# Other due times and ranks for the first five blocks of a fused retention and feed-forward kernel

## The chip, the cores and the metric

The kernel runs on one core of one Trainium2 chip. The metric is the device time of one execution in microseconds (us), the median over several runs. The profile shows one execution; in it PE is the matrix engine, DVE the vector engine, ACT the scalar engine, POOL the general engine, SP the engine that only issues DMAs, and a q behind an engine's name marks its instruction sequencer.

## The reference

```python
scores = scale * np.matmul(q, k.transpose(0, 1, 3, 2))        # 8 batches, 8 heads, 576 tokens, 64 wide
gamma = 1.0 - 2.0 ** (-5.0 - np.arange(H, dtype=np.float32))
rel = pos[:, None] - pos[None, :]
Dmat = np.where(rel >= 0, gamma[:, None, None] ** rel[None, :, :], 0.0)
attn = np.matmul(scores * Dmat[None], v)
x = attn.transpose(0, 2, 1, 3).reshape(4608, 512)
h = x @ w_in                                                  # 512 x 2048
g = np.where(h > 0.0, h, np.exp(np.minimum(h, 0.0)) - 1.0)
out = g @ w_out                                               # 2048 x 512
```

Inputs and output are float32; the kernel multiplies in bfloat16.

## The kernel before

**The work.** Retention runs in chunks of 64 tokens with a running state per head. The 4608 tokens are cut into items of 256 tokens. The four items of the first two batches are cut once more, into two halves by heads; these eight pieces are the units 0 to 7. Each unit has three loads, q, k and v (256 KB each): `ldq4`, `ldk4` and `ldv4` are those of unit 4. From them come scaled and cast copies (`cq` q times its decay, `kk` k cast, `vs` v times its decay), transposed operands, scores with a mask (`mask`), a state (`us`, `ub`) and the transposed input `xt` of the feed-forward part (`xc`). Units 0 to 4 are transposed by PE (`T4_0`, `T4_1`) and copied out of PSUM (`cp`); units 5 to 7 by a DMA transpose on SP's queue (`tr5`, `tr6`, `tr7`; line 594). `A4` to `A7` are the joined PE steps of units 4 to 7: scores and state of this unit, values of the one before.

**The feed-forward part** runs in blocks of 256 tokens. `F1_b_p` is eight matmuls of block b against `w_in`; ACT takes the exponential (`ex`), ACT or DVE the rectified half (`md`), DVE joins them (`g`); `F2_b_t_f` is four matmuls against `w_out`. Blocks 0 and 1 need units 0 to 3, block 2 units 4 and 5, block 3 units 6 and 7.

**The weights.** `w_in` comes in five DMAs (`wi0` to `wi4`, line 486) and `w_out` in four (`wo0` to `wo3`, 512 KB each in bfloat16, line 497), all issued by POOL, with a cast on the way. All other loads are issued by SP in one fixed order (line 392; one early load by ACT). Two loads are held until a quarter of `w_out` is there: POOL copies one element of that quarter into the load's target (line 403), and SP's load waits for this copy. As SP works in order, all loads behind `ldq4` wait with it.

```python
HOLD = {"ldq4": "wo0", "ldq6": "wo1"}
```

**The order.** A list of operations is laid out by a planner inside the kernel while it is built: each operation has a cost on each engine that can do it, a rank, and optionally a due time (`AT`, in us) before which the planner doesn't place it. The planner picks engine and order; the chip then runs each engine's instructions strictly in this order, held only by semaphores. Due times themselves don't exist on the chip. Where the planner sees a gap on PE in the first 50 us, it puts in dummy matmuls on zeros (`zero`, lines 280 and 1273) as filling.

Of the kernel before, what the change touches and what calls it, by code (L numbers as in the profile page):

```python
# [227 lines left out]
UAPART = (5, 7)  # L228
HOLD = {"ldq4": "wo0", "ldq6": "wo1"}
VLATE = (0, 1)  # L230
AT = {"wi0": 7.1, "wi1": 8.0, "wi2": 8.5, "wi3": 11.0, "wi4": 15.0, "wo0": 16.4, "wo1": 16.1, "wo2": 19.3, "wo3": 31.3, "so_0_1_0_0": 74, "so_1_0_0_0": 74, "so_1_1_0_0": 74, "so_2_0_0_0": 76, "so_2_1_0_0": 81.47, "F2_3_1_0_0": 78.57, "g_2_6": 63.17, "md_3_3": 66.87, "md_1_7": 35.82, "us5_0": 44.11, "ex_2_4": 55.85, "ex_2_2": 53.77, "xc1_u4": 43.93, "xc0_4": 82.16, "g_1_3": 27.7, "xc1_u3": 22.43, "F2_3_0_8_0": 78.02, "md_0_7": 36.11, "F1_6_6": 119.86, "tr0_5": 66.58, "md_2_2": 56.94, "ex_6_5": 119.61, "md_0_1": 21.97, "mask1_7": 117.16, "md_0_5": 25.96, "F2_4_0_8_0": 93.26, "cv7": 47.1, "F1_0_5": 22.04, "cq11": 5.73, "ub5_1": 47.68, "F1_0_3": 19.14, "g_1_7": 36.97, "vs1_7": 47.23, "cq00": 4.92, "cq16": 39.58, "ex_0_3": 22.04, "kk1_4": 33.96, "tr6": 42.78, "md_1_0": 25.42}
RANKS = {"us1_0": -2, "F1_0_1": 4, "mask0_7": 2, "g_2_1": -2, "md_3_3": 8, "A7": -4, "cv1_5": -4, "cv1_6": 4, "mask1_u6": 8, "so_5_0_0_0": -8, "md_0_2": -8, "ex_2_7": 2, "xc0_u7": -8, "F1_2_6": -8, "A4": 2, "F2_3_0_4_0": -8, "ub0_0": -4, "kk1_2": 4, "g_0_5": 4, "F2_1_1_0_0": 8}
FREE = ("f", "e", "em", "g", "ot")
SURE = 3
ATT = ((0, 0), (0, 1), (1, 0), (1, 1), (2, 0), (2, 1), (3, 0), (3, 1), (4, 0), (4, 1), "X",
# [12 lines left out]
def kernel(  # L248
# [997 lines left out]
    for op, name in holds:  # L1246
        op.deps.append(named[name])
    for name, t in AT.items():
        if name in named:
            named[name].early = t  # L1250
    for name, shift in RANKS.items():
        if name in named:
# [59 lines left out]
```

## Time and profile before

| what | us |
|---|---|
| median of 3 runs | 298.61 (298.08 to 298.75) |
| the profiled execution | 298.65 |
| its span, first to last instruction | 296.9 |
| PE busy in the span | 289.6 (98%) |
| DVE, ACT, POOL busy | 200.7, 160.1, 119.8 |

The profiled execution's own time is 1.75 us above its span; that part lies outside the instructions. A row of the timeline reads: start, duration, engine, line, operation, tiles, shapes, count, and in brackets the idle time before it with what ended it. A row of the windows gives for each stretch the busy time of each engine, then the clock granted to PE (1.00 is full), the mean busy share of the 16 DMA engines (it passes 1 where packets of several queues overlap) and GB/s. A row of the chain of waits gives start, duration and what the end of the program waited for then.

### The profile page before, as it was taken

How to read it: one execution, taken by the hardware profiler on the slowest of the kernel's cores; microseconds unless marked ns; L12 is line 12 of the kernel's file. 1: busy time of each engine (PE TensorE's matmuls, PEld its weight loads, DVE VectorE, ACT ScalarE, POOL GpSimd, SP SyncE). 2: the span in 40 equal slices, each digit the busy share in tenths (PEclk: the TensorE clock that was granted, in tenths of full speed). 3: DMA queues.
4: the chain of work that ended last, by engine and by line, in shares of the span. 5: the costliest groups of instructions: out<-in, count | busy, mean ns of one | idle time of the engine just before them, and what ended most of it. 6: DMA issues, size and time to landing. Idle time of an engine off the chain costs nothing.

```text
span 296.9 us, 9161 instructions
## 1 busy us (share of the span) xinstructions
PE 289.6 (98%) x3825; PEld 186.8 (63%) x3825; DVE 200.7 (68%) x374; ACT 160.1 (54%) x299; POOL 119.8 (40%) x193
## 2 busy tenths in 40 slices
PE   7999998999999999999999999999999999999995
PEld 4778644776585866776666677767666444444444
DVE  3878831987775878787786867767876567766500
ACT  5568615774283745656565466454565548544311
POOL 5932675763836544565456347370720000000000
PEclk9999999999999999999999999999999999999999
DMA  7999989999999985799999699976461100011221
GB/s 227 283 207 208 285 230 221 263 243 197 291 241 216 270 191 119 187 233 229 239 202 245 127 230 235 244 131 178 112 109 38 38 35 35 0 38 38 50 91 72
DMA packets 128618, 50.67 MB, mean 171 GB/s; under 512 B 92608, under 2 KB 124096, under 8 KB 128576
## 3 DMA queue, kind: packets, MB, share of 16 engines
q1 hardware_dynamic: 123296, 45.63, 67.4%
q0 software_dynamic: 4752, 4.19, 8.8%
q8 instruction: 30, 0.49, 0.7%
q10 hardware_dynamic: 528, 0.26, 0.3%
q14 instruction: 12, 0.10, 0.1%
HBM read 36.70 MB, written 9.44 MB: 155 GB/s over the span
## 4 chain that ended last, share of the span: by engine, by line
PE 82%; DMA 12%; POOL 3%; SPq 1%; issue 1%; ACT 0%; POOLq 0%; ACTq 0%
PE f L280 82%; DMA r<-in_q_dram 4%; DMA w_out_sb<-in_moe_w_out_dram 4%; DMA r<-in_v_dram 2%; DMA T<-st 2%; POOL w_in_sb L486 1%; POOL vn L582 1%; SPq L392 1%; POOL st L559 1%; SPq L594 0%; ACT ot L1179 0%; POOL r L403 0%; POOLq L559 0%; POOL pos_i L515 0%; ACTq L1179 0%
## 5 line engine op out<-in xcount | busy, mean ns | idle before, releaser
L280 PE MATMUL f<-xt,w_in_sb 128*128 128x256 bf16 (+1 forms) x1024 | 140.1, 286 | 0.3 <-DMA w_in_sb<-in_moe_w_in_dram 0.3
L280 PE MATMUL f<-w_out_sb,g 128*128 128x512 bf16 (+1 forms) x592 | 140.2, 373 | 0.0
L1118 ACT ACTIVATE e<-f 128x512 f32<-128x512 f32 x144 | 85.3, 598 | 76.1 <-PE f L280 74.7
L280 PEld LDWEIGHTS <-w_in_sb 128*128 128x128 bf16 x1024 | 99.4, 98 | 37.6 <-DMA w_in_sb<-in_moe_w_in_dram 0.6
L280 PEld LDWEIGHTS <-g 128*128 128x128 bf16 x592 | 56.7, 98 | 51.4
L1132 DVE TENSOR_SCALAR em<-e 128x512 bf16<-128x512 f32 x84 | 45.0, 538 | 39.5 <-ACT e L1118 39.5
L1142 DVE SCALAR_TENSOR_TENSOR g<-f,em 128x512 bf16<-128x512 f32 x84 | 57.4, 688 | 5.5
L1140 DVE SCALAR_TENSOR_TENSOR g<-e,f 128x512 bf16<-128x512 f32 x60 | 40.3, 681 | 10.0 <-ACT f L1128 9.0
L630 POOL CAST kv<-r 128x512 bf16<-128x512 f32 x28 | 17.0, 629 | 48.7 <-issue 26.5
L1179 ACT COPY ot<-f 128x512 f32<-128x512 f32 (+1 forms) x37 | 21.3, 576 | 26.5 <-PE f L280 26.2
L650 POOL TENSOR_TENSOR kv<-r,gq 128x512 bf16<-128x512 f32 x28 | 29.3, 1067 | 12.7 <-DMA r<-in_q_dram 12.7
L650 POOL TENSOR_TENSOR kv<-r,gk 128x512 bf16<-128x512 f32 x28 | 29.5, 1063 | 8.5 <-DMA r<-in_k_dram 8.5
L1128 ACT ACTIVATE f<-f 128x512 f32<-128x512 f32 x54 | 32.2, 598 | 0.0
L1001 ACT CAST xt<-f 128x512 bf16<-128x512 f32 (+1 forms) x36 | 20.7, 624 | 19.5 <-PE f L280 19.4
L969 DVE TENSOR_TENSOR pt<-f,mask 128x512 bf16<-128x512 f32 x28 | 18.0, 679 | 3.0 <-PE f L280 3.0
L954 POOL CAST bd<-S 128x256 bf16<-128x256 f32 x41 | 16.0, 405 | 9.8 <-ACT S L940 5.1
L942 DVE TENSOR_TENSOR S<-f,S 128x256 f32<-128x256 f32 x36 | 15.1, 419 | 3.2 <-PE f L280 1.2
L965 DVE TENSOR_TENSOR pt<-f,mask_u 128x512 bf16<-128x512 f32 x16 | 10.3, 682 | 8.5 <-PE f L280 8.5
L280 PEld LDWEIGHTS <-kv 64*64 64x64 bf16 x832 | 10.8, 104 | 0.1
L280 PE MATMUL f<-T 64*64 64x64 bf16 (+1 forms) x576 | 9.6, 199 | 1.2 <-DMA T<-st 1.2
L559 POOL TENSOR_TENSOR st<-r,gq 128x256 bf16<-128x256 f32 x14 | 8.8, 645 | 4.0 <-DMA r<-in_q_dram 3.9
L280 PEld LDWEIGHTS <-T 64*64 64x64 bf16 x576 | 7.3, 108 | 2.3 <-DMA T<-st 1.4
(67 smaller groups left out, 123.5 us busy)
## 6 DMA issues: line engine op xcount, KB each, us to landing
r<-in_v_dram SPq DMA_DIRECT2D x32, 256.0 KB, 4.5
r<-in_k_dram SPq DMA_DIRECT2D x31, 256.0 KB, 4.3
out_dram<-ot SPq DMA_DIRECT2D x31, 256.0 KB, 2.9
r<-in_q_dram SPq DMA_DIRECT2D x12, 512.0 KB, 4.6
r<-in_q_dram SPq DMA_DIRECT2D x8, 256.0 KB, 4.3
w_out_sb<-in_moe_w_out_dram POOLq DMA_DIRECT2D x4, 512.0 KB, 11.5
w_in_sb<-in_moe_w_in_dram POOLq DMA_DIRECT2D x3, 512.0 KB, 9.1
out_dram<-ot SPq DMA_DIRECT2D x10, 128.0 KB, 2.2
```

Of the source, the lines that this page charges most:

```text
L280: return pin(nc.tensor.matmul(*a, **kw))
L630: pin(copy[op.eng](heads(tiles[nkey][:, VS[s]]), tiles["rv", n][:, s * H : (s + 1) * H]))
L650: pin(alu[op.eng].tensor_tensor(tiles[nkey][:, 2 * i + j].rearrange("p (y x d) -> p x y d", y=2, x=HP), raw.rearrange("p (x y) d -> p x y ...
L954: pin(copy[op.eng](tiles[bkey], tiles[skey]))
L969: pin(nc.vector.tensor_tensor(pt.rearrange("p h s n -> p (h s) n"), src.rearrange("p (h n) -> p h n", n=C), mask.rearrange("p e r -> p (e ...
L1001: pin(copy[op.eng](dst, src))
L1118: pin(nc.scalar.activation(tiles[ekey], tiles[hkey], AF.Exp))
L1128: pin(nc.scalar.activation(ph, ph, AF.Relu))
L1132: pin(alu[op.eng].tensor_scalar_add(em, e, -1.0))
L1140: pin(nc.vector.scalar_tensor_tensor(g, e, -1.0, ph, ALU.add, ALU.min))
L1142: pin(nc.vector.scalar_tensor_tensor(g, ph, 0.0, tiles[mkey], ALU.max, ALU.min))
L1179: pin(copy[op.eng](tiles[okey][:, :width], tiles[pkey][:, :width]))
```

## The change

Only the two tables of due times and ranks differ, and of them only entries of the first five blocks and units 0 to 7. `HOLD` is as it was.

```diff
-AT: "wi2": 8.5, "wo0": 16.4, "wo1": 16.1, "wo2": 19.3, "wo3": 31.3, "F1_0_3": 19.14
+AT: "wi2": 8.8, "wo0": 16.7, "wo1": 15.8, "wo2": 19.9, "wo3": 31.1
+AT: "ub4_1": 43.87, "T0_0": 8.14, "md_0_0": 19.36, "xc0_u0": 13.99, "T4_0": 35.06,
+    "cp1_1": 10.22, "md_0_3": 23.9, "kk0_0": 5.92, "cp4_1": 38.78
+RANKS: "xc1_u1": 4, "md_0_3": -2, "md_1_4": -2, "F1_1_0": 8, "cp4_0": 2, "tr7": -8, "cq17": 2, "g_1_6": 8
```

What this does to the instructions of each engine:

- POOL: before, `wo0`, `wo1`, `wo2` were issued in this row, then came the hold of `ldq4` (on `wo0`), ten small operations that make tables, the hold of `ldq6` (on `wo1`), and `wo3`. Now `wo1` is issued first, then `wo0` and `wo2`; the tables come next, then both holds together, then `wo3`. So `ldq4` waits for the second quarter that is issued instead of the first, and `wo3` stands directly behind both holds. Further on, `ub4_0` moves behind `cq16` and `kk1_6`, and `ub4_1` behind the two `cq` of unit 7. Early on, POOL and DVE exchange some `vs` and `cq` of units 0 to 3, and POOL takes two casts `ub` from ACT.
- SP: the same order.
- PE: units 0 to 3 are interleaved otherwise (unit 1's transposes first), one `F1` step instead of two stands ahead of the last steps of units 2 and 3, `F1_1_0` comes behind the next three; `T4_0` moves behind two `F2` steps to stand with `T4_1`, and `A4` behind one `F2` step. Fourteen more dummies stand ahead of the first transposes, and ten more in all. From the step behind `A4` on, the order is the same to the end.
- ACT and DVE: of the eight copies `cp` of units 0 to 3 six are on ACT instead of two, both of unit 4 are on DVE, and the `ex`, `md`, `g` of blocks 0 and 1 stand in another order. From unit 4's mask on, both are the same.

More of the change, by code (lines that the diff above doesn't have):

```diff
@@ L230 @@
 VLATE = (0, 1)
-AT = {"wi0": 7.1, "wi1": 8.0, "wi2": 8.5, "wi3": 11.0, "wi4": 15.0, "wo0": 16.4, "wo1": 16.1, "wo2": 19.3, "wo3": 31.3, "so_0_1_0_0": 74, "so_1_0_0_0": 74, "so_1_1_0_0": 74, "so_2_0_0_0": 76, "so_2_1_0_0": 81.47, "F2_3_1_0_0": 78.57, "g_2_6": 63.17, "md_3_3": 66.87, "md_1_7": 35.82, "us5_0": 44.11, "ex_2_4": 55.85, "ex_2_2": 53.77, "xc1_u4": 43.93, "xc0_4": 82.16, "g_1_3": 27.7, "xc1_u3": 22.43, "F2_3_0_8_0": 78.02, "md_0_7": 36.11, "F1_6_6": 119.86, "tr0_5": 66.58, "md_2_2": 56.94, "ex_6_5": 119.61, "md_0_1": 21.97, "mask1_7": 117.16, "md_0_5": 25.96, "F2_4_0_8_0": 93.26, "cv7": 47.1, "F1_0_5": 22.04, "cq11": 5.73, "ub5_1": 47.68, "F1_0_3": 19.14, "g_1_7": 36.97, "vs1_7": 47.23, "cq00": 4.92, "cq16": 39.58, "ex_0_3": 22.04, "kk1_4": 33.96, "tr6": 42.78, "md_1_0": 25.42}
@@ L232 @@
-RANKS = {"us1_0": -2, "F1_0_1": 4, "mask0_7": 2, "g_2_1": -2, "md_3_3": 8, "A7": -4, "cv1_5": -4, "cv1_6": 4, "mask1_u6": 8, "so_5_0_0_0": -8, "md_0_2": -8, "ex_2_7": 2, "xc0_u7": -8, "F1_2_6": -8, "A4": 2, "F2_3_0_4_0": -8, "ub0_0": -4, "kk1_2": 4, "g_0_5": 4, "F2_1_1_0_0": 8}
+AT = {"wi0": 7.1, "wi1": 8.0, "wi2": 8.8, "wi3": 11.0, "wi4": 15.0, "wo0": 16.7, "wo1": 15.8, "wo2": 19.9, "wo3": 31.1, "so_0_1_0_0": 74, "so_1_0_0_0": 74, "so_1_1_0_0": 74, "so_2_0_0_0": 76, "so_2_1_0_0": 81.47, "F2_3_1_0_0": 78.57, "g_2_6": 63.17, "md_3_3": 66.87, "md_1_7": 35.82, "us5_0": 44.11, "ex_2_4": 55.85, "ex_2_2": 53.77, "xc1_u4": 43.93, "xc0_4": 82.16, "g_1_3": 27.7, "xc1_u3": 22.43, "F2_3_0_8_0": 78.02, "md_0_7": 36.11, "F1_6_6": 119.86, "tr0_5": 66.58, "md_2_2": 56.94, "ex_6_5": 119.61, "md_0_1": 21.97, "mask1_7": 117.16, "md_0_5": 25.96, "F2_4_0_8_0": 93.26, "cv7": 47.1, "F1_0_5": 22.04, "cq11": 5.73, "ub5_1": 47.68, "g_1_7": 36.97, "vs1_7": 47.23, "cq00": 4.92, "cq16": 39.58, "ex_0_3": 22.04, "kk1_4": 33.96, "tr6": 42.78, "md_1_0": 25.42, "ub4_1": 43.87, "T0_0": 8.14, "md_0_0": 19.36, "xc0_u0": 13.99, "T4_0": 35.06, "cp1_1": 10.22, "md_0_3": 23.9, "kk0_0": 5.92, "cp4_1": 38.78}
@@ L233 @@
+RANKS = {"us1_0": -2, "F1_0_1": 4, "mask0_7": 2, "g_2_1": -2, "md_3_3": 8, "A7": -4, "cv1_5": -4, "cv1_6": 4, "mask1_u6": 8, "so_5_0_0_0": -8, "md_0_2": -8, "ex_2_7": 2, "xc0_u7": -8, "F1_2_6": -8, "A4": 2, "F2_3_0_4_0": -8, "ub0_0": -4, "kk1_2": 4, "g_0_5": 4, "F2_1_1_0_0": 8, "xc1_u1": 4, "md_0_3": -2, "md_1_4": -2, "F1_1_0": 8, "cp4_0": 2, "tr7": -8, "cq17": 2, "g_1_6": 8}
 FREE = ("f", "e", "em", "g", "ot")
```

## The prediction

> **What bounds the kernel now.** The page comes first: PE is busy for nearly the whole span, at full clock.
>
> ```profile
> span 296.9 us, 9161 instructions
> PE 289.6 (98%) x3825; PEld 186.8 (63%) x3825; DVE 200.7 (68%) x374; ACT 160.1 (54%) x299; POOL 119.8 (40%) x193
> PEclk9999999999999999999999999999999999999999
> ```
>
> A share over the whole span doesn't say what an earlier start is worth, so I read the chain of waits next, in order of time.
>
> ```profile
> 15.35 10.53 DMA w_out_sb<-in_moe_w_out_dram
> ...
> 26.15 5.93 DMA r<-in_q_dram
> ...
> 44.40 6.29 DMA T<-st
> 50.69 0.04 issue
> 50.73 8.02 PE f L280 x152
> 58.75 0.04 issue
> 58.79 171.01 PE f L280 x2692
> 229.80 0.04 issue
> 229.84 63.76 PE f L280 x356
> ```
>
> From 50.73 us to 293.60 PE runs through; the pieces are parted only by 0.04 us. All of this work is the same after the change, in the same order. So whatever the change does, the end moves by as much as the step at 50.73 moves, as long as nothing behind it comes late. That step is `A6`; it waited for the DMA transpose `tr6`, issued at 44.40 and landed 6.29 us later. The chain also shows where loads begin: the first quarter of `w_out` lands at 15.35 + 10.53 = 25.88, and q of unit 4 is issued at 26.15.
>
> Now PE ahead of that, from its timeline:
>
> ```profile
> 14.87 1.91 PE L280 MATMUL f<-xt,w_in_sb 128*128 128x256 bf16 x16
> ...
> 21.15 1.05 PE L280 MATMUL f<-xt,w_in_sb 128*128 128x256 bf16 x8 [0.28 <-DMA w_in_sb<-in_moe_w_in_dram]
> 22.04 0.28 PE L280 MATMUL f<-zero 128*128 128x128 bf16 x2
> ...
> 23.08 8.90 PE L280 MATMUL f<-xt,w_in_sb 128*128 128x256 bf16 x80
> ...
> 35.49 0.39 PE L605 MATMUL f<-ident,st 128*128 128x128 bf16 x4
> ...
> 42.43 0.32 PE L280 MATMUL f<-vn,st 64*64 64x64 bf16 x16
> ...
> 48.53 1.04 PE L280 MATMUL f<-xt,w_in_sb 128*128 128x256 bf16 x8
> 50.73 0.42 PE L280 MATMUL f<-T 64*64 64x128 bf16 x16 [1.16 <-DMA T<-st]
> ```
>
> PE stands in front of `A6` at 48.53 + 1.04 = 49.57 and idles 1.16 us. There are thus two runners to 50.73: PE with the work of blocks 0 and 1, which has 1.16 us in hand, and the loads with `tr6`, which have none. A delay of PE below 1.16 us costs nothing; a shift of `tr6` counts in full for a delay, and up to 1.16 us for a gain, where PE becomes the later one.
>
> **The loads' runner, part by part.** What does `tr6` hang on? SP's queue and POOL:
>
> ```profile
> 27.11 0.51 SPq L392 DMA_DIRECT2D r<-in_v_dram  x1
> ...
> 38.90 1.96 SPq L594 DMA_TRANSPOSE T<-st  x1
> ...
> 42.10 2.13 SPq L392 DMA_DIRECT2D r<-in_v_dram  x3
> 44.40 2.76 SPq L594 DMA_TRANSPOSE T<-st  x1
> ```
>
> ```profile
> 25.93 0.19 POOL L403 CAST r<-w_out_sb 128x1 f32<-128x1 bf16 x1 [8.28 <-DMA w_out_sb<-in_moe_w_out_dram]
> 28.84 0.19 POOL L403 CAST r<-w_out_sb 128x1 f32<-128x1 bf16 x1 [0.81 <-DMA w_out_sb<-in_moe_w_out_dram]
> 29.30 0.79 POOL L497 DMA_DIRECT2D w_out_sb<-in_moe_w_out_dram  x1 [0.26 <-issue]
> 34.29 0.39 POOL L568 CAST st<-r 128x256 bf16<-128x256 f32 x1
> 38.13 0.74 POOL L568 CAST st<-r 128x256 bf16<-128x256 f32 x2 [1.72 <-DMA r<-in_k_dram]
> 41.32 0.29 POOL L904 CAST s<-mid 128x128 bf16<-128x128 f32 x1
> ```
>
> `tr6` is issued as soon as SP has done `tr5` and the five loads behind it (42.10 + 2.13 = 44.23). `tr5` starts at 38.90, when POOL's two casts of k of unit 5 end (38.13 + 0.74 = 38.87), and these waited for the landing of `ldk5`. SP's order is unchanged. So the question is one number: when does `ldk5` land, 38.1 us before?
>
> The new hold of `ldq4`: it waits for the quarter issued second. Before, that one was there by 28.84, 2.9 us behind the first. So `ldq4` is issued at about 28.6 to 29.0 instead of 26.15, up to 2.9 us later, and with it all SP loads behind it. The hold of `ldq6` then passes at once, and `wo3` is issued at about 29.1 instead of 29.30. That is all it does to `wo3`: its place behind the hold of `ldq6` is the old one.
>
> Do the 2.9 us come through to `ldk5`? The windows of 1 us show what the DMA engines did in that time:
>
> ```profile
> 26.00:27.00 1.00, 1.00 (x11) 0.90 (x10) 1.00 (x3) 0.95 (x3) 0.76 (x7) 1.00 1.25 204
> 28.00:29.00 1.00, 1.00 (x12) 0.90 (x10) 1.00 (x3) 1.00 (x4) 0.19 (x2) 1.00 1.26 205
> 29.00:30.00 1.00, 1.00 (x12) 0.90 (x10) 1.00 (x3) 1.00 (x3) 0.74 (x2) 1.00 1.18 244
> 30.00:31.00 1.00, 1.00 (x12) 0.90 (x10) 1.00 (x2) 1.00 (x3) 0.09 (x1) 1.00 1.16 320
> 31.00:32.00 1.00, 1.00 (x10) 0.82 (x9) 1.00 (x3) 1.00 (x3) 0.00 (x0) 1.00 1.15 341
> ```
>
> At 26 to 27, before a load can move, the weights alone give 204 GB/s at a busy share of 1.25. At 28 to 29, with q, k and v of unit 4 issued (v at 27.11), it is still 205: the loads waiting there got next to nothing. Only from 29 on does the rate rise towards 341, that is, loads run on engines that have done their share of the third quarter. So the 2.9 us that `ldq4` loses are mostly time in which it waited anyway. What it loses is at most what moved above 205 GB/s from 29 to 31: 39 + 115 = 154 KB, at 341 GB/s 0.45 us. That is the upper bound of the direct cost. The lower: the engines have the same bytes to move up to `ldk5`, they aren't idle in any of these windows, and `wo3` comes 0.2 us sooner; the last engine to finish decides the landing, and it would lose nothing, or even win 0.2 us. Between -0.2 and +0.45 I take +0.1: the row nearest to it is the busy share, 1.15 to 1.26 throughout, which leaves little room for a loss on the slowest engine.
>
> The Trainium skill, DMA: Bandwidth & Descriptors, section Queues, rings and completion order, has each DMA engine take turns between the queues that have work, a packet at a time. By that rule loads waiting beside weights get turns, and a load let go 2.9 us later gives its turns up. The trace speaks mostly against a large share here (205 GB/s at 28 to 29); by the rule, the sum would lean to its upper end and to the slower case below.
>
> Casts: `ub4_0` ran at 41.32, and stands now behind one `cq` and one `kk`, 1 us later, done by about 42.6. It feeds `A5`, which began at 42.43: up to 0.3 us of waiting on PE, hidden in the 1.16. In turn `cq16` and `kk1_6`, which `tr6` needs, end 0.25 us sooner; that gains nothing, as `tr6` stood behind SP's own loads till 44.23.
>
> **PE's runner.** Early units: DVE's first mask came at 7.68. Now nine operations (three `vs`, two `cq`, two `us`, a `cp`, a `ub`) stand between the landing of v, at 7.00, and that mask:
>
> ```profile
> 7.00 0.42 DVE L582 TENSOR_TENSOR vn<-r,gk 128x256 bf16<-128x256 f32 x1 [0.54 <-DMA r<-in_v_dram]
> ...
> 7.68 1.29 DVE L965 TENSOR_TENSOR pt<-f,mask_u 128x512 bf16<-128x512 f32 x2
> ```
>
> Nine at up to 0.42, and less for the narrow ones, put it at about 10.4, 2.7 us later. But then four masks run in a row at 1.29 per two, and `F1_0_0` waits only for the values of unit 1: from 10.4, 2.6 for four masks, some 0.6 for the values and 1.3 for ACT's and PE's steps between, gives 14.9 to 15.4 against 14.87. Behind it, from 14.87 to 23.08, PE spent 8.21 us with 0.28 idle and about 0.2 on dummies. The new order has one `F1` less ahead of units 2 and 3 and no such gap, as `wi3` is there by then (it freed the step at 21.15). So 14.9 to 15.4 plus 7.7 gives 22.6 to 23.1: between 0.5 sooner and level. I take 0. The fourteen dummies ahead of the first transposes fill a wait for the loads.
>
> `T4_0` and `T4_1` stand together where `T4_1` stood, at 35.49. They need the second cast of k of unit 4, at 34.29 + 0.39 = 34.68: 0.8 us in hand. If `ldq4` lands 0.45 later they are still in time; 1 us later costs PE 0.2, covered. `A4` behind one more `F2` only exchanges two steps. The exchanged `F1`, `ex`, `md`, `g` are the same work on engines that kept PE fed without a gap from 23.08; zero.
>
> **The sum.** `tr6` +0.1; PE 0 to +0.5, under the 1.16: `A6` at 50.83, the end +0.1. The profiled execution took 298.65, so 298.75; the median of the runs shown is 298.61, 0.04 below it, and I keep 298.75. A measurement of this kernel can tell about 0.2%, 0.6 us, from no change.
>
> **The rivals.** *Slower: the late hold comes through.* If the loads' 2.9 us aren't mostly waste, `ldk5` lands later, and each tenth goes straight to `A6`. For it: the loads did move from 29 to 31, and with `ldq4` issued at 28.8 and a normal landing time
>
> ```profile
> r<-in_q_dram SPq DMA_DIRECT2D x8, 256.0 KB, 4.3
> ```
>
> it lands at 33.1 instead of 26.15 + 5.93 = 32.08, 1.0 us later; then `wo3` meets more waiting loads than before. Against it: the full engines. Price 0.7 to 1.5 us, say 1.1: 299.75. It decides from 38.7 for the landing of `ldk5`, 0.6 late. Chance 0.28.
>
> *Faster: the loads win.* The landing of `wo3`, from the answer on its tile in that window:
>
> ```profile
> DMA to landing us min/median/max: 8.6/8.6/8.6
> ```
>
> Without loads between them the quarters of `w_out` land sooner, `wo3` goes out earlier, and loads then run back to back; `ldk5`, which landed only just behind `wo3` (29.30 + 8.6 = 37.9), comes up to 1.16 us sooner, and PE runs through. For it: 1.16 us of idle PE stand there to be won, and mixing slows the weights (2.9 us between two quarters, against 512 KB at 205 GB/s, 2.6 us). Against it: the bytes ahead of `ldk5` are the same. Price up to 1.16: 297.5. Chance 0.18.
>
> *The change doesn't do what it says:* the place of `wo3` on POOL is the same in both; its new due time only moves the plan. That is part of the likeliest case.
>
> **How the numbers follow.** No change that can be told: 0.54, with 298.2 to 299.3 as its own range. The range reaches to both rivals' prices, 297.5 and 299.9; beyond it I leave some 0.15, most of it above. Faster by over 0.2% 0.18, within 0.54, slower 0.28.
>
> **What would show it.** Right: the hold of `ldq4` ends at 28.4 to 28.9 with that of `ldq6` right behind it, the casts of k of unit 5 start at 37.9 to 38.6, `tr6` is issued at 44.2 to 44.9, and `A6` starts at 50.5 to 51.2 with PE idle ahead of it. Wrong: `ldk5` beyond 38.7; or PE arriving at `A6` after 50.7, because of late masks of the early units, `T4_1` or `A5`; or a new gap of PE behind 50.73.

## The result: 1.4% slower, and the profile after

The changed kernel takes 302.60 us (median of 6, 301.35 to 304.33), the kernel before, in runs beside it, 298.35 (median of 6): ratio 1.0144, 95% interval 1.0107 to 1.0181. The forecast was 298.75 with a range to 299.9. Ratios here and below leave out the few executions in a slower state of the chip, while medians are of all, so the two can differ a little. The mean granted clock of the changed kernel's six executions lies between 0.987 and 1.00; the two at 1.00 took 301.35 and 302.33, so 3 to 4 us of the loss are there without a lowered clock. The profiled execution took 303.34 at a mean clock of 0.992, its span is 301.6.

The page of the changed kernel:

```profile
span 301.6 us, 9175 instructions
PE 292.1 (97%) x3835; PEld 188.2 (62%) x3835; DVE 199.9 (66%) x375; ACT 159.6 (53%) x297; POOL 119.7 (40%) x194
PEclk9999979999999999999999999999999999999999
```

The sixth slice of the clock, 37.7 to 45.2 us, reads 7 where all others read 9. The chain of waits, start and duration:

```profile
29.10 6.76 DMA r<-in_k_dram
...
38.86 0.62 POOL vn L582
39.48 0.35 POOL st L568
...
40.16 23.32 PE f L280 x312
...
63.53 170.94 PE f L280 x2693
234.47 0.04 issue
234.51 63.76 PE f L280 x356
```

The work of the long stretch of PE is the same as before, but it comes later, and what leads to it is no longer the transpose of unit 6. It is k of unit 4 (issued at 29.10), POOL's scaling of v (38.86) and its second cast of k (39.48). PE's timeline:

```profile
20.66 11.53 PE L280 MATMUL f<-xt,w_in_sb 128*128 128x256 bf16 x104
32.02 3.62 PE L280 MATMUL f<-w_out_sb,g 128*128 128x512 bf16 x16
35.48 0.39 PE L605 MATMUL f<-ident,st 128*128 128x128 bf16 x4
36.38 0.28 PE L605 MATMUL f<-ident,st 128*128 128x128 bf16 x2 [0.52 <-DVE T L611]
39.88 0.29 PE L605 MATMUL f<-ident,st 128*128 128x128 bf16 x2 [3.21 <-POOL st L568]
40.00 5.30 PE L280 MATMUL f<-w_out_sb,g 128*128 128x512 bf16 x16
...
54.50 1.04 PE L280 MATMUL f<-xt,w_in_sb 128*128 128x256 bf16 x8
55.47 0.42 PE L280 MATMUL f<-T 64*64 64x128 bf16 x16
```

Two things stand here. `T4_1` idles 0.52 + 3.21 = 3.73 us, in two parts, as its four transposes wait for the two casts of k (the first row names DVE's copy, which ended with POOL's first cast at 36.32). And sixteen `F2` matmuls take 5.30 us right behind it, where the sixteen at 32.02 took 3.62: 1.68 us more. `A6` starts at 55.47 without idling, against 50.73 before with 1.16 idle. The account: 3.73 + 1.68 - 1.16 = 4.25, and 0.2 for a later start of `F2` (32.02 against 31.81 before), of 4.74; some 0.3 is not assigned. It holds for this execution; the two at full clock can't have had the 1.68.

The row of `F2` before:

```profile
31.81 1.89 PE L280 MATMUL f<-w_out_sb,g 128*128 128x512 bf16 x8
```

POOL, which issues the quarters and casts k and v:

```profile
28.48 0.31 POOL L403 CAST r<-w_out_sb 128x1 f32<-128x1 bf16 x2 [8.45 <-DMA w_out_sb<-in_moe_w_out_dram]
29.03 0.79 POOL L497 DMA_DIRECT2D w_out_sb<-in_moe_w_out_dram  x1 [0.24 <-issue]
31.79 1.18 POOL L559 TENSOR_TENSOR st<-r,gq 128x256 bf16<-128x256 f32 x2 [1.97 <-DMA r<-in_q_dram]
35.92 0.40 POOL L568 CAST st<-r 128x256 bf16<-128x256 f32 x1 [2.96 <-DMA r<-in_k_dram]
38.86 0.62 POOL L582 TENSOR_TENSOR vn<-r,gk 128x256 bf16<-128x256 f32 x1 [2.54 <-DMA r<-in_v_dram]
```

```profile
28.69 0.37 SPq L392 DMA_DIRECT2D r<-in_q_dram  x1
```

Both holds end together at 28.5 to 28.8, and `wo3` goes out at 29.03, 0.34 us behind `ldq4` (28.69; before it was 3.15 us behind). q of unit 4 is there at 31.8 (32.1 before). k comes at 35.9, and v at 38.8, just behind `wo3` (29.03 + 9.4 = 38.4). The windows say how the DMA engines spent that time, and what the clock did (third value from the end):

```profile
29.00:30.00 1.00, 1.00 (x12) 0.89 (x10) 1.00 (x3) 1.00 (x3) 0.79 (x1) 1.00 1.00 178
30.00:31.00 1.00, 1.00 (x12) 0.90 (x10) 1.00 (x3) 1.00 (x3) 0.00 (x0) 1.00 1.02 258
31.00:32.00 1.00, 1.00 (x11) 0.90 (x10) 1.00 (x3) 1.00 (x3) 0.21 (x1) 1.00 1.01 246
32.00:33.00 1.00, 1.00 (x7) 0.50 (x6) 1.00 (x3) 1.00 (x3) 0.97 (x2) 1.00 0.75 103
...
41.00:42.00 1.00, 1.00 (x5) 0.37 (x3) 0.00 (x0) 0.00 (x0) 1.00 (x3) 0.53 0.91 275
43.00:44.00 1.00, 1.00 (x3) 0.30 (x2) 0.00 (x0) 0.00 (x0) 1.00 (x3) 0.50 0.51 118
```

And before, behind the stretches that the prediction shows:

```profile
32.00:33.00 1.00, 1.00 (x6) 0.49 (x5) 0.89 (x2) 1.00 (x3) 0.77 (x2) 1.00 1.21 311
```

From 29 to 33 the changed kernel moved 178 + 258 + 246 + 103 = 785 KB, the kernel before 244 + 320 + 341 + 311 = 1216 KB. The engines were part empty: the share was 1.00 to 1.02 and fell to 0.75, where it had been 1.15 to 1.21. (A share above 1 is no sign of several queues here: with the weights alone it was 1.25 at 26 to 27.)

### The profile page after: what moved, and what is told of

The parts are those of the page before. It is cut to its first block, busy times and chain, and to the rows that moved or that the text cites. A ratio compares the mean times of both kernels' runs of the same rounds, so it can differ in the third digit from the quotient of the medians.

```text
span 301.6 us, 9175 instructions
## 1 busy us (share of the span) xinstructions
PE 292.1 (97%) x3835; PEld 188.2 (62%) x3835; DVE 199.9 (66%) x375; ACT 159.6 (53%) x297; POOL 119.7 (40%) x194
## 4 chain that ended last, share of the span: by engine, by line
PE 86%; DMA 8%; POOL 3%; issue 1%; SPq 1%; ACT 0%; POOLq 0%; ACTq 0%
PE f L280 86%; DMA w_out_sb<-in_moe_w_out_dram 4%; DMA r<-in_k_dram 2%; DMA r<-in_v_dram 2%; POOL vn L582 1%; SPq L392 1%; POOL w_in_sb L486 0%; POOL st L559 0%; POOL st L568 0%; POOL w_out_sb L497 0%; POOL s L904 0%; PE f L605 0%; ACT ot L1179 0%; PE f L1273 0%; POOL r L403 0%
## 5 line engine op out<-in xcount | busy, mean ns | idle before, releaser
L280 PE MATMUL f<-w_out_sb,g 128*128 128x512 bf16 (+1 forms) x592 | 141.7, 377 | 0.0
L1132 DVE TENSOR_SCALAR em<-e 128x512 bf16<-128x512 f32 x84 | 43.7, 522 | 39.5 <-ACT e L1118 39.5
L965 DVE TENSOR_TENSOR pt<-f,mask_u 128x512 bf16<-128x512 f32 x16 | 10.4, 684 | 10.2 <-PE f L280 10.2
L559 POOL TENSOR_TENSOR st<-r,gq 128x256 bf16<-128x256 f32 x12 | 7.6, 650 | 4.2 <-DMA r<-in_q_dram 4.2
L582 POOL TENSOR_TENSOR vn<-r,gk 128x256 bf16<-128x256 f32 x12 | 7.6, 644 | 3.3 <-DMA r<-in_v_dram 3.3
```

Source lines behind the costliest of these rows:

```text
L280: return pin(nc.tensor.matmul(*a, **kw))
L1132: pin(alu[op.eng].tensor_scalar_add(em, e, -1.0))
```

## Experiments

Theory A: `wo3`, issued close behind `ldq4`, catches the loads of unit 4. Rival B: the late release of `ldq4` costs by itself. Rival C: the new order of the early units, of `T4` and `A4` costs. All edits but two move entries of the finished order, so that POOL's list changes in one place (in two in a_both); the tables of due times stay. "Before" in a ratio is the kernel before in runs beside it.

**Exchange the quarters in the changed kernel (a_wo0first).**

```diff
     order = plan.run({"PE": 1.3, "DVE": 2.2, "ACT": 0.8, "POOL": 4.4, "SP": 0.8})
+    a, b = order.index(named["wo0"]), order.index(named["wo1"])
+    order[a], order[b] = order[b], order[a]
```

> The changed kernel with wo0 and wo1 exchanged on POOL and nothing else moved: ldq4 is held by the quarter issued first again, while wo3 still stands right behind both holds. Theory A (wo3 catches the loads of unit 4: it was issued 0.3 us behind ldq4 in the changed kernel, 3.2 us behind it before): ldq4 goes out at about 26, 3 us ahead of wo3, k and v of unit 4 land by 34, no wait of PE at T4_1; 298.0 to 299.0. Rival B (the late release itself costs, whatever wo3 does): the same, 298 to 299. Rival C (the new order of the early units, of T4 and A4 costs): still 301.5 to 303.

298.0 us, ratio 0.9981 (0.9949 to 1.0014). The whole loss is gone with this one exchange, and with all the rest of the new order in place. That ends rival C; A and B both expected it. PE runs through `T4_0` and `T4_1` without idling:

```profile
35.45 0.61 PE L605 MATMUL f<-ident,st 128*128 128x128 bf16 x8
```

**The same exchange in the kernel before (b_wo1first).** The edit is the same two lines. Here the tables stay between the holds.

> The kernel before with wo0 and wo1 exchanged on POOL: ldq4 is held by the second quarter, released at about 28.5, but the tables still stand between its hold and wo3, so wo3 goes out at about 30.8, 2 us behind it. Theory A: most of unit 4 is through before wo3; k of unit 4 lands by 33.5, v by 33.5 to 36, PE waits 0 to 1 us at T4_1; 298.3 to 299.5. Rival B (late release): as slow as the changed kernel, 301.5 to 303. Rival C: no change, 298.4.

300.43, ratio 1.0076 (1.0041 to 1.0112): between A and B. `T4_1` didn't wait (36.69), yet PE idled 2 us at `A5`, for the transpose of unit 5, and the clock fell behind that too:

```profile
45.98 0.42 PE L280 MATMUL f<-T 64*64 64x128 bf16 x16 [1.98 <-DMA T<-st]
...
47.00:48.00 1.00, 1.00 (x5) 0.42 (x4) 0.80 (x3) 0.95 (x4) 1.00 (x3) 0.50 1.27 290
```

`tr5` was issued at 39.44, 0.5 us later than before, but took 6.5 us to land. The profiled execution, 302.46, is one of the longest of ten (299.54 to 302.60). PE also idled 0.78 us at 31.26 for DVE's `g`, which stood behind the late tables; that gap is no part of the loss, as `A5` had to wait for `tr5` anyway. So a late release costs something also with `wo3` 2.2 us behind it, by a way that neither theory had named.

**`wo3` close behind `ldq4`, without a late release (b_wo3early).**

```diff
+    order.remove(named["wo3"])
+    order.insert(order.index(named["holdldq4"]) + 1, named["wo3"])
```

> The kernel before with wo3 moved on POOL from behind the hold of ldq6 to right behind the hold of ldq4: the release of ldq4 stays at 26, but wo3 is issued 0.4 us behind it. Theory A: the quarters run on without a pause to about 34, the loads of unit 4 land between 34 and 38, PE waits 2 to 4 us at T4_0 or T4_1; 300.5 to 303. Rival B and rival C: 298 to 299, as neither the release nor the order of the other work has changed.

300.09, ratio 1.0067 (1.0028 to 1.0106): A's direction, just below its range. POOL shows the loads of unit 4 caught: the first cast of k at 35.83 (before 33.36), the second at 37.16, 2.9 us later than before.

```profile
26.39 0.76 POOL L497 DMA_DIRECT2D w_out_sb<-in_moe_w_out_dram  x1
...
35.83 0.40 POOL L568 CAST st<-r 128x256 bf16<-128x256 f32 x1 [0.54 <-DMA r<-in_k_dram]
...
37.16 0.40 POOL L568 CAST st<-r 128x256 bf16<-128x256 f32 x1
```

In its profiled execution the clock had fallen early, from 8.4 to 18.6 us, so PE itself came late and the wait at `T4_1` can't be read from it. The early fall isn't all of the loss: the shortest of its ten executions took 299.24, that of the kernel before 297.26.

**`wo3` late in the changed kernel (a_wo3late).** `wo3` is put behind `cq14` in the same way.

> The changed kernel with wo3 moved on POOL behind the two cq of unit 4, which wait for q of unit 4, so that wo3 goes out at about 33 instead of 29; the late release of ldq4 at 28.7 stays. Theory A: k and v of unit 4 land at 32.5 to 34, PE doesn't wait at T4_1; wo3 lands at about 41.5, ahead of its first use at 44; 297.5 to 299. Rival B: 301.5 to 303. Rival C: 301.5 to 303.

300.2, ratio 1.0068 (1.0034 to 1.0102). A expected 299 at most and was wrong, though k and v of unit 4 were in time and `T4` didn't wait. In the profiled execution, 298.80, the wait had moved on to `A5`:

```profile
43.65 0.24 PE L280 MATMUL f<-T,s 64*64 64x128 bf16 x2 [1.06 <-POOL s L904]
```

Its chain goes from here over POOL's casts of unit 6 to the landing of `ldk6` (33.70 + 8.29 = 41.99), which `wo3`, issued at 33.2 and landed at 40.8, seems to have held up. But this execution is the shortest of ten (to 301.72), and its `A6` starts where it did before, so what the median lost is in no trace:

```profile
50.72 0.42 PE L280 MATMUL f<-T 64*64 64x128 bf16 x16
```

**Keep PE's clock up (a_dummies).**

```diff
+            if op.name == "T4_1":
+                for n in range(52):
+                    pin(nc.tensor.transpose(tiles[fresh[0]][:, n % 4], zero[:, :P], ident))
```

> The changed kernel with 52 dummy transposes of zeros on PE ahead of T4_1, some 3 us of them, so that PE doesn't stand idle while it waits for k of unit 4; nothing else moved. Theory (the wait of 3.7 us lets the granted clock fall to 0.5 for some 3.5 us, which costs another 1.7 us): the clock stays at 1.00 from 36 to 46, the first 16 F2 matmuls behind T4_1 take 3.6 us instead of 5.3, and the time falls by 1 to 2 us, 300.5 to 301.6. Rival (the slow stretch is the wait's own, dummies only take its place): 302 to 303.

301.41, ratio 1.0115 (1.0091 to 1.0139). PE waits as long for k, but works on zeros meanwhile, and the sixteen `F2` behind it take 3.62 us at full clock instead of 5.30:

```profile
39.60 0.28 PE L605 MATMUL f<-ident,st 128*128 128x128 bf16 x2 [0.55 <-POOL st L568]
39.72 3.62 PE L280 MATMUL f<-w_out_sb,g 128*128 128x512 bf16 x16
...
41.00:42.00 1.00, 1.00 (x6) 0.49 (x5) 0.00 (x0) 0.00 (x0) 1.00 (x4) 1.00 0.66 197
```

That the clock takes 1.7 us in an execution where it falls is thus shown by the profile. How much of the 4.25 us between the medians is the clock's is less sure: 1.2 by the medians, 0.9 by the ratios, whose intervals overlap.

**Let k past v on POOL (a_kkfirst).** `kk1_4` is put behind `kk0_4`, ahead of `vs0_4`.

> The changed kernel with the second cast of k of unit 4 (kk1_4) moved on POOL ahead of the scaling of v (vs0_4) that waits for v of unit 4. Theory (T4_1 waits for v, which it doesn't use, only because POOL works in order): T4_1 follows the landing of k of unit 4 at about 36, PE idles about 1 us there instead of 3.7 and keeps its clock; the end is then set by what is late next, the transposes of unit 5 (landed at 45.1) and 6 (52.2): 299 to 300.8. Rival (k itself is the late one): 302 to 303.

299.71, ratio 1.0057 (1.0035 to 1.0078): 2.9 us less than the changed kernel. `T4_1` now follows k and idles 0.82, and the clock stays at 1.00. What is left of the loss isn't divided between the release and `wo3`: POOL's work ahead of `A5` still ran late behind k and v of unit 4, which landed at 35.7 and 37.8.

```profile
36.25 0.63 PE L605 MATMUL f<-ident,st 128*128 128x128 bf16 x4 [0.82 <-POOL st L568]
...
44.19 0.24 PE L280 MATMUL f<-T,s 64*64 64x128 bf16 x2 [0.44 <-POOL s L904]
```

**The hold ahead of the tables in the changed kernel (a_tables).** `holdldq4` is put behind `wo2`, so `wo3` goes out at 31.16, 2.2 us behind `ldq4`, with the late release kept.

> The changed kernel with the hold of ldq4 moved on POOL ahead of the tables: the release stays at 28.7 (second quarter), but wo3 goes out at about 31 instead of 29, 2 us behind ldq4. Theory (two costs: the late release some 2 us, wo3 close behind ldq4 another 2 us with the clock): the second goes, no wait at T4_1, the first stays as a wait at A5 for the transpose of unit 5, 299.5 to 301. Rival (wo3's distance doesn't matter): 302 to 303. Rival (the late release alone costs nothing in this order): 297.5 to 298.7.

299.56, ratio 1.0033 (1.0005 to 1.0061). The wait at `T4_1` is gone. PE idles 0.87 and 0.16 us as DVE's `g` now stand behind the late tables, which this edit made, and 0.58 at `A5`, for POOL's cast and not for the transpose that was expected. Only `A5` counts, since the chain to POOL's cast hangs on loads and not on PE: it ran over v of unit 5, which landed at 41.3 (38.8 before), with `wo3` in flight till 41.2.

```profile
31.13 1.03 PE L280 MATMUL f<-xt,w_in_sb 128*128 128x256 bf16 x8 [0.87 <-DVE g L1140]
...
44.71 0.24 PE L280 MATMUL f<-T,s 64*64 64x128 bf16 x2 [0.58 <-POOL s L904]
```

**`wo3` late in the kernel before (b_wo3late1).** `wo3` is put behind `kk0_4`.

> The kernel before with wo3 moved on POOL behind the first cast of k of unit 4, issued at about 33.5 instead of 29.3; the release of ldq4 stays at 26. Theory (a quarter of w_out holds up the loads that are waiting when it starts): the loads of unit 5 now land ahead of wo3, ldk5 at about 36 instead of 38.1, tr5 and tr6 go out 1 to 2 us sooner, PE doesn't wait at A6; wo3 lands at about 42, ahead of its first use at 44: 296.8 to 298.2. Rival (the loads behind unit 5 are then held up instead and tr6 with them): 298 to 299.5.

300.12, ratio 1.0034 (0.9998 to 1.0069): not the gain that was expected. `tr5` went out 1 us sooner, at 37.92, as `ldk5` was no longer caught. But it landed only at 44.50, behind `wo3` (33.69 + 9.9 = 43.6). The chain and PE:

```profile
37.92 6.58 DMA T<-st
44.50 0.04 issue
44.54 5.48 PE f L280 x71
```

```profile
44.54 0.42 PE L280 MATMUL f<-T 64*64 64x128 bf16 x16 [1.48 <-DMA T<-st]
```

This fits b_wo1first too: `wo3` landed at 40.7 there, and `tr5`, issued at 39.44, took 6.5 us. In a_wo0first and in the changed kernel `wo3` had landed when `tr5` was issued, and it took 3.3 and 2.8.

**Release still sooner (b_early).** The emitted hold of `ldq4` reads the last quarter of `w_in` instead of `wo0`.

```diff
+                    at_ = "wi4" if name == "ldq4" else behind
-                    i = int(behind[2:])
+                    i = int(at_[2:])
```

> The kernel before with the hold of ldq4 on the last quarter of w_in (landed at 23.3) instead of the first of w_out (25.9), so that ldq4 goes out 2.5 us sooner. Theory (late loads leave the DMA engines part empty at 29 to 33): sooner loads keep them full, the loads of units 4 and 5 land up to 1 us sooner and tr6 with them; w_out lands 1 to 2 us later without anyone waiting: 297 to 298.3. Rival (loads beside the weights only take from the weights): within 0.3 of the kernel before; or F2 waits for w_out and it is 298.5 to 300.

298.7, ratio 1.0017 (0.9989 to 1.0045): no gain. `ldq4` went out at 23.78 instead of 26.15, and k and v of unit 4 landed at 33.7 and 34.5, no sooner than in a_wo0first (32.8 and 33.6). The loads that were let go earlier only waited longer beside the weights.

**Repeated, and with a second edit (a_best, a_both, b_kkfirst).** a_best is a_wo0first again. a_both adds `kk1_4` ahead of `vs0_4`. b_kkfirst is that last edit alone in the kernel before.

> The changed kernel with wo0 and wo1 exchanged on POOL once more, in more rounds, to tell it from the kernel before. Theory (all of the loss lies in which quarter holds ldq4; the rest of the new order is neutral): within 0.2% of the kernel before, 297.5 to 298.5. Rival (the rest of the new order is worth something): 297.3 to 297.9, 0.2 to 0.4% below the kernel before.

> The changed kernel with wo0 and wo1 exchanged and kk1_4 ahead of vs0_4 on POOL. If T4_1 has k in time anyway once ldq4 goes out at 26 (theory), the second edit brings nothing: as a_best within 0.3. Rival (v of unit 4 is still what T4_1 waits for in some runs): 0.3 to 1 below a_best, fewer runs with a lowered clock.

> The kernel before with kk1_4 ahead of vs0_4 on POOL, nothing else moved. Theory (k and v of unit 4 are in time at T4_1 there, so this edit alone changes nothing): within 0.2% of the kernel before. Rival (the gain of a_both over a_best comes from this edit): 0.2 to 0.4% faster, and tr6 lands by 49.6 instead of 50.7.

a_best: 298.05, ratio 0.9996 (0.997 to 1.0021). a_both: 297.67, ratio 0.9969 (0.9946 to 0.9992), the only one of the twelve whose interval lies below 1, and only just; with so many compared, one may do so by chance. b_kkfirst: 298.51, ratio 1.0003 (0.9968 to 1.0038), with `A6` idling 0.9 us (1.16 in the kernel before). In the profile of a_both PE doesn't idle at `A6`: `tr6` landed there at 48.3, in a_best at 50.5, with `tr6` issued at the same time (43.8 and 43.7). Which of these a run gets isn't settled: the intervals of a_best and a_both overlap, a_wo0first showed the early landing (48.6) with the edits of a_best, and no run takes apart what makes `tr6` land early.

The runs that move only the release of `ldq4` or the distance of `wo3` behind it, with the landing of k and v of unit 4 and of k of unit 5, from their traces (a dash where the trace has no landing):

| kernel | `ldq4` issued | `wo3` behind it | k, v of unit 4 | k of unit 5 | ratio |
|---|---|---|---|---|---|
| before | 26.15 | 3.15 | -, 33.6 | 38.1 | 1 |
| a_wo0first | 26.40 | 2.85 | 32.8, 33.6 | 37.9 | 0.9981 |
| b_early | 23.78 | 6.45 | 33.7, 34.5 | 39.0 | 1.0017 |
| b_wo3late1 | 26.35 | 7.34 | 32.8, 33.6 | 35.1 | 1.0034 |
| b_wo3early | 26.37 | 0.02 | 35.8, 36.5 | 37.9 | 1.0067 |
| a_tables | 28.91 | 2.25 | 32.8, 34.3 | 38.8 | 1.0033 |
| b_wo1first | 29.04 | 2.24 | 32.9, 34.4 | 38.6 | 1.0076 |
| a_wo3late | 29.00 | 4.23 | 32.7, 34.2 | 35.8 | 1.0068 |
| changed | 28.69 | 0.34 | 35.9, 38.8 | - | 1.0144 |

k and v of unit 4 come 2 us late or more only where `wo3` stands within 0.4 us of `ldq4`; a late release with `wo3` farther behind leaves them within 0.8 us of before, and `wo3` then meets loads or transposes of units 5 and 6. Either fault costs 0.3 to 0.8% in these runs, both together 1.4%. (b_wo3late1 has neither; its interval reaches 1.)

## Why the prediction was wrong

**The steps that held.** The holds: forecast at 28.4 to 28.9 with `wo3` at about 29.1, measured 28.48 and 29.03. That the end moves as `A6` moves: 4.74 at `A6`, 4.7 in the span. That the new order of the early units is neutral: `F1_0_0` began at 15.73 instead of the 14.9 to 15.4 worked out, but `F2` only 0.2 us later than before, and a_wo0first and a_best are level with the kernel before.

**The step that failed first** is "the question is one number: when does `ldk5` land". The loads' runner had an earlier check point, `T4_1`. The prediction looked at it, gave it 0.8 us in hand, and charged it only with the slip of q (0.45, or 1.0). q did land in time, and `T4_0`, which turns q and not k, ran at 35.48. But `T4_1` turns k, and the second cast of k ended at 39.82 instead of 34.68, 5.1 us late. For k and v of unit 4 stand behind q, and the rate falls towards that of the weights (204 to 210 GB/s) some 3 to 4 us behind the issue of `wo3` (before: issued at 29.30, 311 GB/s at 32 to 33 and 233 at 33 to 34; a_wo3late: issued at 33.23, 343 at 35 to 36 and 204 at 37 to 38). In the new order only q was through by then. Before, 3.15 us lay between, enough for all three. The sentence that let this by is "That is all it does to `wo3`": it set the issue of `wo3` against its own old time, not against the release of the loads. The distance of two issues on two queues was in the quoted rows (26.15, 29.30, and the 28.6 to 29.1 worked out for after) and wasn't taken as a quantity. POOL's order made it worse: the second cast of k stood behind v, which `T4_1` doesn't use. a_kkfirst measures this part, with the clock that hangs on it, at 2.9 us. Among its signs of being wrong the prediction had a late PE because of `T4_1`, but no term for it.

**The second** is "the engines aren't idle in any of these windows", from which came the upper bound of 0.45 us. The busy shares quoted were those of the kernel before, where loads stood ready. With the loads held 2.5 us longer there was less for the engines to fill in: 785 KB instead of 1216 KB from 29 to 33, which at 341 GB/s is 1.3 us of lost transfer. Most of that goes with the release, as a_wo3late, whose `wo3` went out only at 33.2, moved 119 + 204 + 310 + 216 = 849 KB in the same stretch. Why the share fell to 0.75 at 32 to 33, with k and v of unit 4 still outstanding, no run shows. The landing of `ldk5`, which the sum had 0.1 us late, isn't in the trace of the changed kernel; q of unit 5 ahead of it landed at 39.6 and v behind it at 41.1, so it was 1.5 to 3 us late if it kept that order. With the same release and `wo3` it landed at 40.0 in a_dummies and 39.3 in a_kkfirst, beyond the 38.7 that was to decide for the slower case. And `ldk5` isn't all: in b_wo1first it came 0.5 us late, near the bound, and still the kernel lost 2.3 us, as `tr5` took 6.5 us to land.

**The third** is the cover. PE's 1.16 us in hand were right, and are in the account. But a wait beyond them had a price of its own that was not in the sum: the clock. It read 0.50 from 41.1 to 44.4, behind 3.7 us of near idleness, and cost 1.7 us more in the profiled execution. The Trainium skill, TensorE: Matmul & The Clock Gate, Part 1, says that the matrix engine falls to half clock after an idle window of about 3.4 us and comes back after one as long. The trace agrees with the half, and with the time back here and in b_wo1first (46.3 to 49.7), but b_wo1first fell to 0.50 behind an idle of only 1.98, and b_wo3early stayed at 0.50 for 10.2 us (8.4 to 18.6) with PE busy nearly all the time. Behind idles of 1.06 (a_wo3late) and 1.48 (b_wo3late1) the clock stayed at 1.00.

The slower rival had the direction and the kind of cause ("`wo3` meets more waiting loads than before"), and was priced at 1.1 us instead of 4.3, for the same two reasons. The rule set beside the trace, turns between queues from the Trainium skill, DMA: Bandwidth & Descriptors, Queues, rings and completion order, leaned to this case. The runs bear out the case, but not a gain from early turns: b_early shows none from 2.4 us of them, and with `wo3` in flight v, issued at 29.66, landed only at 38.8, just behind `wo3`.

## What to carry to other kernels

Where loads and large weights share the DMA engines, write down for every pair the distance from the release of the loads to the issue of the next weight, and count how many loads fit in; an exchange that moves neither list much can close that distance. Check the earliest user of each load, and what stands ahead of it on in-order engines, not only the user that was late before. A busy share read in the old profile holds only as long as something is queued; and once the matrix engine idles for 2 us or more, as in the two waits here of 1.98 and 3.73 us behind which the clock halved, add the time at half clock to the wait. It can also fall without such a wait: in b_wo3early no idle of PE from 5 us to the fall at 8.4 was above 0.37.

## What the runs showed of the hardware

The DMA transpose `tr5` took 4.7 to 6.6 us to land where a quarter of `w_out` was in flight when it was issued (a_tables 4.7, a_wo3late 5.9, b_wo1first 6.5, b_wo3late1 6.6), and 2.8 to 3.7 in eight runs where the quarter had landed. The quarter is not the only thing that can lengthen a transpose: `tr6`, with none in flight, took 4.2 to 6.8 us. And issuing on SP's queue can itself take long: with five loads outstanding and `wo3` in flight, issuing one load (`ldq6`) of the changed kernel took 4.69 us, and everything behind it on SP waited. It took 3.82 us in a_kkfirst and 3.14 in a_dummies, and 0.86 in the kernel before.

```profile
33.34 4.69 SPq L392 DMA_DIRECT2D r<-in_q_dram  x1
```
